# Block products in the down projection of the last four token tiles, and one scale per weight

## The chip, the cores and the metric

The kernel runs on one core of a Trainium2 chip. A core has a matrix engine (PE), a vector engine (DVE), an engine for functions (ACT), a general one (POOL) and one that mostly issues transfers (SP). Each works through its own list of instructions in order and waits, where it must, for what another engine or a transfer delivers. The metric is the device time of one execution in microseconds (us). Before the change it was 216.23 us, the median of three runs (215.68 to 216.25).

## The reference

The input x has S = 2048 tokens of D = 512 features. The kernel must give

```
xn  = layernorm(x)
out = x + linear_attention(xn) @ wo + ((xn @ w_gate) * (xn @ w_up)) @ w_down
```

in bfloat16. w_gate and w_up are 512 x 1792, w_down is 1792 x 512. The attention has 32 heads of 16 features: q, k and v come from wqkv; q and k pass a small matrix per head (w_phi) and become the feature map softmax(p) and softmax(-p); phi_k and v are summed over all tokens to one 32 x 17 block per head (the 17th column is the sum of phi_k); each token's phi_q times that block gives a numerator and a denominator, and their quotient goes through wo.

## The kernel before

The 2048 tokens are 16 tiles of 128, in groups of four. The 1792 hidden features are 14 slices of 128, the 512 features four. The code switches the framework's scheduler off: the order in which the code issues instructions is the order on each engine, transfers on SP among them.

The stages in time are these.

- *0 to about 88 us.* Layernorm and transposes; for the first eight tiles, gate and up are plain matmuls (`ffn`, L344 to L372), interleaved with the projections of k and v, their features and the sums KV. `weight_norm` (L417) has ACT sum the absolute values of each block of w_gate and w_up.
- *88 to 110 us.* `attend(n)` (L683) multiplies phi_q of tile n by KV into a PSUM bank `ab` that exists once; DVE then makes the denominator `den`, its reciprocal `rden` and the quotient `otok`, and SP transposes that to `oT`. `attend(n + 1)` cannot start until DVE has read `ab` of tile n. `qproj` makes q of a tile: PE's matmul, two exponentials on ACT, a reduction and a reciprocal on DVE (L300, L302), the product `phiq` on POOL (L304), and a transpose by SP. `fin(n)` (L374 to L406) is the last step of a tile: 14 rows (matmuls) with the slices of w_down and four with wo into one bank, then `store` adds x on DVE (L398) and sends the tile out.
- *110 to about 173 us.* Gate and up of tokens 1024 to 2047 are not plain products. For a pair of token groups and a pair of hidden slices, the 2 x 2 block product of activations and weights is made by seven block products in place of eight (`pair_block`, L467 to L540; `run_blocks`, L704). They need sums and differences of weights (`weight_sums`, L437, one 512-column subtraction each, on POOL or DVE, L445) and of tokens (`token_sums`, L449). Both are kept in fp16, so weights are first multiplied by a power of two (`weight_up`, L433), found from the norms in `weight_scales` (L422); `both` undoes it for each of seven pairs of slices. Block i (0 to 13) is gate or up of pair k. In a gate block, ACT copies partial sums out of PSUM with that scale (`keep`, L493) and DVE joins them (L499). In an up block ACT copies without scale (L495), DVE adds (L503) and the result is multiplied into the stored gate (L504): on POOL for the first six pairs, on DVE for the last. Rows of `fin` for tiles 4 to 7 and the q of tiles 7 to 12 fill PE between the products.
- *173 to 214 us.* The last block, then `fin` of tiles 8 to 15. Ahead of `fin(n)` for n = 9, 10, 11 stand q of tile n + 4 and `attend(n + 1)`. Tile 15 is done in two cuts, of 384 and 128 columns.

PSUM has eight banks: six turn over in one pool, and two are `ab` in the second and last stages, and banks for `fin` and q in the third.

The loop of the last stage sets the order around the change:

```
for n in range(9, NT):
    if n < 12:
        q_begin(n + 4, bank)
        q_rest()
    if n + 1 < NT:
        attend(n + 1, ps_ab)
    if sends:
        qsend()
    if n < 12:
        q_features(True)
    fin(n, cuts=(0, D) if n < NT - 1 else (0, 3 * P, D))
```

Of the kernel before, what the change touches and what calls it, by code (L numbers as in the profile page):

```python
# [23 lines left out]
def kernel(  # L24
# [49 lines left out]
    wgu = wpool.tile([P, 2, DC, F], BF16)  # L74
# [60 lines left out]
    xnT = xpool.tile([P, DC, HALF], BF16)  # L135
# [238 lines left out]
    def fin_parts(n, new_bank, lo=0, hi=D):  # L374
# [28 lines left out]
    def fin(n, cuts=(0, D)):  # L403
        for lo, hi in zip(cuts, cuts[1:]):
            for part in fin_parts(n, bank, lo, hi):
                part()  # L406

    nrm = consts.tile([P, FH, 2], BF16)
    up2 = consts.tile([P, FH, 2], F32)
    down2 = consts.tile([P, FH, 2], F32)  # L410
    both = consts.tile([P, FH], F32)
# [10 lines left out]
    def weight_scales():  # L422
        flat = lambda t: t[:].rearrange("p k g -> p (k g)")
        ps = bank("nrm")[:, 0:2 * FH]
        nc.tensor.matmul(ps, lhsT=ones[:, 0:P], rhs=flat(nrm), start=True, stop=True)
        nc.vector.tensor_scalar(out=flat(up2), in0=ps, scalar1=2.0 ** -40, scalar2=None, op0=ALU.max)
        nc.vector.tensor_scalar(out=flat(up2).bitcast(I32), in0=flat(up2).bitcast(I32), scalar1=0x7F800000,
                                scalar2=None, op0=ALU.bitwise_and)
        nc.vector.tensor_scalar(out=flat(down2), in0=flat(up2), scalar1=2.0 ** -14, scalar2=None, op0=ALU.mult)
        nc.vector.reciprocal(out=flat(up2), in_=flat(down2))  # L430
        nc.vector.tensor_tensor(out=both[:], in0=down2[:, :, 0], in1=down2[:, :, 1], op=ALU.mult)

    def weight_up(k, g):  # L433
        cols = pair_cols(k)[:, g]
        nc.scalar.activation(out=cols, in_=cols, func=AF.Identity, scale=up2[:, k, g:g + 1])  # L435
# [31 lines left out]
    def pair_block(k, g, new_bank):  # L467
# [7 lines left out]
        for t in range(2):  # L475
            T = NGRP // 2 + t
            if T not in hTs:
                hTs[T] = hpool.tile([P, FC, TT], BF16, name="hT", tag="h")
            for i in range(2):
                h[t, i] = hTs[T][:, k + i * FH, :]  # L480
        f = both[:, k:k + 1]
# [60 lines left out]
    norms = [(k, g) for k in range(FH) for g in range(2)]  # L542
# [61 lines left out]
    with tc.tile_pool(name="ps_k", bufs=1, space=PSUM) as ps_k:  # L604
# [66 lines left out]
        token_sums((0,))  # L671
        ffn(1)
        kv(NT - 2)
        ffn(1)
        kv(NT - 1)
        for b in range(2):
            nc.vector.tensor_tensor(out=KV[:, 4 * b:4 * b + 4, :, :], in0=kvps[b][:],
                                    in1=_bcast_ap(M4[:], [M4[:].ap[0], [0, 4], [E1, 4], [1, E1]]), op=ALU.mult)
        ffn(1)

    dpool = ctx.enter_context(tc.tile_pool(name="dp", bufs=2))

    def attend(n, ps_ab):  # L683
        ab = ps_ab.tile([P, 2, TT], F32, name="ab")
        for gr in range(NG):
# [6 lines left out]
                                scalar2=r2[:, n:n + 1] if n < GT else 1.0, op0=ALU.add, op1=ALU.mult)  # L692
# [11 lines left out]
    def run_blocks(lo, hi, first, second, third):  # L704
        for i in range(lo, hi):
# [7 lines left out]
            if 2 <= i < 2 * FH - 4:  # L713
                weight_up(*blocks[i + 4])
            new["p2"]()
# [12 lines left out]
    with tc.tile_pool(name="ps_ab", bufs=1, space=PSUM) as ps_ab:  # L728
        attend(0, ps_ab)
        weight_scales()  # L730
        qproj(4, True)
        token_sums((1,))
# [18 lines left out]
        qproj(7)  # L751
        weight_sums(1)
# [7 lines left out]
    with tc.tile_pool(name="ps_f", bufs=2, space=PSUM) as ps_f:  # L760
# [11 lines left out]

        def with_q(i):
# [4 lines left out]
                   lambda i: q_rest() if with_q(i) else filler(3 + i // 12))  # L778
        filler(len(fill))

    with tc.tile_pool(name="ps_ab2", bufs=1, space=PSUM) as ps_ab:
        nothing = lambda i: None
# [51 lines left out]
```

## Time and profile before

| | |
|---|---|
| median of three runs | 216.23 us |
| the profiled execution | 215.67 us |
| its span, first instruction to last | 213.9 us |
| clock granted to PE | 1.00 |
| busy: PE, DVE, ACT, POOL | 98%, 76%, 58%, 60% |
| `fin` with w_down, 238 matmuls | 54.1 us |
| transfers, share of 16 engines | 36.6% |

By stage, busy time in us:

| from, to | PE | DVE | ACT | POOL |
|---|---|---|---|---|
| 0 to 88 | 87.07 | 69.11 | 67.27 | 55.29 |
| 88 to 110 | 22.00 | 17.12 | 11.26 | 17.64 |
| 110 to 165 | 54.91 | 46.79 | 38.24 | 45.12 |
| 165 to 184 | 19.00 | 15.94 | 6.07 | 5.31 |
| 184 to 214 | 27.16 | 14.24 | 2.17 | 5.80 |

The profile is one execution, recorded by the hardware. A busy share says how much of the span an engine had an instruction running; the chain that ended last is followed back from the last instruction to whatever released each step. A line such as "0.42 DVE L445 TENSOR_TENSOR T<-wgu 128x512 f16<-128x512 bf16 x2" in a timeline names duration, engine, line of the kernel, operation, result and operands, their shapes and types, and how many instructions were merged. Matmuls overlap, so PE's rate is read from starts, not from durations.

### The profile page before, as it was taken

To read this page: it belongs to the slowest core of one execution; us is meant where nothing else is said; L and a number is where in the kernel's file an instruction comes from. 1 tells how busy PE (TensorE), PEld (TensorE's weight loads), DVE (VectorE), ACT (ScalarE), POOL (GpSimd) and SP (SyncE) were. 2 spreads that over 40 slices of the span, in tenths; PEclk is the share of its full clock that TensorE was granted. 3 is DMA by queue.
4 is the path that set the end of the run, shared out by engine and by line. 5 is a ranking of instruction groups with operands and counts; after the bars stand their busy time and mean duration, and the time that the engine had idled before them with its cause. 6 is when DMAs were issued, how large, how long until landed. Compare 5 with 4: busy or idle time off the path is not lost.

```text
span 213.9 us, 3610 instructions
## 1 busy us (share of the span) xinstructions
PE 210.1 (98%) x1280; PEld 101.7 (48%) x1280; DVE 163.2 (76%) x279; ACT 125.0 (58%) x219; POOL 129.2 (60%) x112
## 2 busy tenths in 40 slices
PE   8999999999999999999999999999999999999994
PEld 3664445444444444554444444444444444444543
DVE  5757979869867788887777897988969689776341
ACT  4635578998896999442666686868746352220000
POOL 3600557597895788859899497979788620333000
PEclk9999999999999999999999999999999999999999
DMA  5999995613022023234444202021120201333511
GB/s 152 266 281 385 374 287 87 91 26 75 0 51 52 0 49 81 66 40 112 100 101 100 49 0 52 0 74 25 48 49 3 74 26 34 91 98 98 126 49 49
DMA packets 47249, 19.91 MB, mean 93 GB/s; under 512 B 37504, under 2 KB 46976, under 8 KB 47104
## 3 DMA queue, kind: packets, MB, share of 16 engines
q1 hardware_dynamic: 47232, 19.69, 36.6%
q8 instruction: 10, 0.16, 0.3%
q14 instruction: 7, 0.06, 0.1%
HBM read 8.67 MB, written 2.10 MB: 50 GB/s over the span
## 4 chain that ended last, share of the span: by engine, by line
PE 98%; ACT 1%; DVE 0%; issue 0%
PE fin L387 29%; PE g L350 11%; PE u L350 11%; PE sa L487 11%; PE pv L285 7%; PE q L285 6%; PE k L285 6%; PE sc L487 6%; PE sb L487 3%; PE kv L622 2%; PE ab L686 2%; PE warm L554 2%; PE pq L272 1%; PE tp L253 1%; ACT k L493 0%; ACT xnT L256 0%
## 5 line engine op out<-in xcount | busy, mean ns | idle before, releaser
L387 PE MATMUL fin<-wd,hT 128*128 128x512 bf16 (+2 forms) x238 | 54.1, 366 | 0.0
L304 POOL TENSOR_TENSOR phiq<-e,rs 128x1024 bf16<-128x1024 f32 x16 | 30.9, 1934 | 25.6 <-DVE rs L302 18.1
L304 POOL TENSOR_TENSOR phik<-e,rs 128x1024 bf16<-128x1024 f32 x16 | 30.9, 1933 | 24.2 <-DVE rs L302 17.3
L300 DVE TENSOR_REDUCE sums<-e 128x64 f32<-128x1024 f32 x32 | 38.7, 1208 | 9.0 <-ACT e L296 9.0
L350 PEld LDWEIGHTS <-wgu 128*128 128x128 bf16 x240 | 23.1, 98 | 24.2
L387 PEld LDWEIGHTS <-hT 128*128 128x128 bf16 x238 | 22.3, 98 | 24.4
L350 PE MATMUL u<-xnT,wgu 128*128 128x512 bf16 (+1 forms) x120 | 29.1, 365 | 0.0
L350 PE MATMUL g<-xnT,wgu 128*128 128x512 bf16 (+1 forms) x120 | 28.9, 365 | 0.0
L504 POOL TENSOR_TENSOR hT<-u_sb,hT 128x512 bf16<-128x512 bf16 x18 | 21.1, 1185 | 10.1 <-DVE u_sb L503 10.1
L362 DVE TENSOR_TENSOR hT<-u,g_sb 128x512 bf16<-128x512 f32 (+1 forms) x30 | 18.6, 622 | 4.5 <-PE u L350 3.9
L356 ACT CAST g_sb<-g 128x512 bf16<-128x512 f32 (+1 forms) x30 | 17.1, 569 | 8.1 <-PE g L350 7.9
L294 ACT ACTIVATE e<-q 128x512 f32<-128x512 f32 x12 | 7.2, 598 | 23.6 <-PE q L285 23.6
L302 DVE RECIPROCAL rs<-sums 128x64 f32<-128x64 f32 x32 | 17.7, 552 | 2.5
L493 ACT ACTIVATE k<-sa,both 128x512 f32<-128x512 f32 x21 | 14.5, 688 | 8.7 <-PE sa L487 8.6
L495 ACT COPY k<-sa 128x512 f32<-128x512 f32 x21 | 12.3, 587 | 11.2 <-DVE u_sb L503 7.4
L398 DVE TENSOR_TENSOR o_sb<-fin,xall 128x512 bf16<-128x512 f32 (+2 forms) x13 | 8.4, 646 | 12.0 <-PE fin L387 12.0
L445 POOL TENSOR_TENSOR T<-wgu,T 128x512 f16<-128x512 bf16 x14 | 17.0, 1216 | 0.5
L387 PE MATMUL fin<-wo,oT 128*128 128x512 bf16 (+2 forms) x68 | 17.1, 366 | 0.0
L487 PEld LDWEIGHTS <-T 128*128 128x128 f16 x112 | 10.8, 98 | 13.1 <-issue 0.6
L487 PE MATMUL sa<-ss,T 128*128 128x512 f16 x56 | 16.7, 379 | 0.1
L435 ACT ACTIVATE wgu<-wgu,up 128x1024 bf16<-128x1024 bf16 x14 | 15.9, 1156 | 0.1
L420 ACT ACTIVATE junk<-wgu 128x1024 bf16<-128x1024 bf16 x14 | 15.1, 1083 | 0.0
(98 smaller groups left out, 352.1 us busy)
## 6 DMA issues: line engine op xcount, KB each, us to landing
out_dram<-o_sb SPq DMA_DIRECT2D x15, 128.0 KB, 1.9
wd<-in_B_w_down_dram SPq DMA_DIRECT2D x1, 1792.0 KB, 15.4
wgu<-in_B_w_gate_dram SPq DMA_DIRECT2D x2, 640.0 KB, 6.8
wgu<-in_B_w_up_dram SPq DMA_DIRECT2D x2, 640.0 KB, 8.0
xall<-in_A_x_dram SPq DMA_DIRECT2D x1, 1024.0 KB, 12.1
xall<-in_A_x_dram SPq DMA_DIRECT2D x4, 128.0 KB, 2.7
vk<-in_A_wqkv_dram SPq DMA_DIRECT2D x2, 256.0 KB, 3.6
wgu<-in_B_w_gate_dram SPq DMA_DIRECT2D x2, 256.0 KB, 4.9
```

The lines of the kernel that those rows point to most:

```text
L285: nc.tensor.matmul(ps, lhsT=xt(n)[:, j, :], rhs=w[:, j, :], start=(j == 0), stop=(j == DC - 1))
L300: nc.vector.tensor_reduce(out=sums[:], in_=ev, axis=AX.X, op=ALU.add)
L302: nc.vector.reciprocal(out=rs[:].rearrange("p a b -> p (a b)"), in_=sums[:])
L304: nc.gpsimd.tensor_tensor(out=phi[:].rearrange("p g (x f) -> p (g x) f", f=DH), in0=ev, in1=rs[:].to_broadcast((P, 2 * H, DH)), op=ALU.mult)
L350: nc.tensor.matmul(ps, lhsT=w[:, c, f * P:(f + 1) * P], rhs=xnT[:, c, T * TT + lo:T * TT + hi], start=(c == 0), stop=(c == DC - 1))
L356: nc.scalar.copy(out=g_sb[:, 0:n], in_=ps)
L362: nc.vector.tensor_tensor(out=hTs[T][:, f, lo:hi], in0=ps, in1=g_sb[:, 0:hi - lo], op=ALU.mult)
L387: nc.tensor.matmul(held[0], lhsT=rows[i][0], rhs=rows[i][1], start=(i == 0), stop=(i == len(rows) - 1))
L435: nc.scalar.activation(out=cols, in_=cols, func=AF.Identity, scale=up2[:, k, g:g + 1])
L445: (nc.gpsimd if i % 2 or k < 2 else nc.vector).tensor_tensor(out=t[:, i], in0=a, in1=b, op=ALU.subtract)
L487: nc.tensor.matmul(held[name], lhsT=w[:, j, :], rhs=x[:, j, :], start=start and j == 0, stop=(j == hc - 1), skip_group_check=True)
L504: (nc.vector if k == FH - 1 else nc.gpsimd).tensor_tensor(out=dst, in0=u[:], in1=dst, op=ALU.mult)
```

## The change

*w_down of tiles 12 to 15.* They are taken as two pairs, (12, 13) and (14, 15). For a pair, the activations are a 2 x 2 block matrix (two tiles by two halves of the 1792 hidden features), w_down another (two halves of the hidden features by two halves of its 512 columns). The product is made by seven block products of seven matmuls with 256 columns each (`down_pair`, p1 to p7, p2 of the last pair in halves p2a and p2b, plus `w22`, which has only rows of wo) and 16 rows of wo, in place of two `fin`.

*What the products need.* All quarters of w_down in fp16, multiplied by a power of two (`scaled`, on ACT, 12 pieces of 768 or 1024 columns, six in blocks 5 to 10 and six in and after the last block); four differences of quarters (`minus`, 16 pieces of 512 or 256 columns, all on POOL: one at block 10, three at 11, four at 12, the rest in the last stage); and four sums or differences of activations per pair (`hidden_sums`, 896 columns each; number 0 and number 6 on POOL, the others on DVE). Inside `down_pair`, `keep` copies partial sums on ACT, `add` adds x or another partial sum on POOL, and `join` finishes a half tile on DVE. The new tiles lie where tiles that are no longer read were: the first w_down pieces over the transposed activations of the first half and over x of tiles 0 to 3, the activation sums over w_gate and w_up.

*Scales.* Gate times up of tokens 1024 to 2047 is stored in fp16 with a fixed factor (`gate_scale`), so the seven factors `both` become one constant. Each weight has one scale, from the root of its sum of squares: `weight_norm` takes squares, with seven more calls for w_down, and `weight_roots`, `weight_scales` and `product_scales` replace the old `weight_scales`. The factors are undone in `store`, in `den` (`scale_of`) and in `down_pair`.

*Order.* q of tile 13 stands ahead of the last two rows of `fin(8)`; three rows of `fin(9)` ahead of `attend(10)`; q of 14 behind `fin(9)`; q of 15 in the middle of `fin(10)`. `attend(14)` and `attend(15)` stand inside the first pair. The first of `token_sums` stands two units of `ffn` later.

```diff
...
-            if n < GT:
-                nc.vector.scalar_tensor_tensor(out=o_sb[:], in0=ps, scalar=r2[:, n:n + 1], in1=xres,
-                                               op0=ALU.mult, op1=ALU.add)
+            if n < GT or n >= QT:
+                nc.vector.scalar_tensor_tensor(out=o_sb[:], in0=ps, scalar=r2[:, n:n + 1] if n < GT else inv_a[:],
+                                               in1=xres, op0=ALU.mult, op1=ALU.add)
             else:
                 nc.vector.tensor_tensor(out=o_sb[:], in0=ps, in1=xres, op=ALU.add)
             nc.sync.dma_start(out=out_view(n, n + 1)[:, 0, lo:lo + w], in_=o_sb[:])
...
     def weight_norm(k, g):
-        junk = xnpool.tile([P, DC, 2, P], BF16, name="junk", tag="x")
+        junk = xnpool.tile([P, 1024], BF16, name="junk", tag="x")
+        cols = pair_cols(k)[:, g] if g < 2 else wd[:, 2 * k:2 * k + 2, :]
+        out = junk[:].rearrange("p (c h f) -> p c h f", c=DC, h=2) if g < 2 else junk[:].rearrange("p (c f) -> p c f", c=2)
         with nc.allow_low_precision(reason="a bound for a power of two"):
-            nc.scalar.activation(out=junk[:], in_=pair_cols(k)[:, g], func=AF.Abs, accum_out=nrm[:, k, g:g + 1])
-
...
+            nc.scalar.activation(out=out, in_=cols, func=AF.Square, accum_out=nrm[:, g, k:k + 1])
...
+    def weight_roots(lo, hi):
+        n = hi - lo
+        ps = bank("nrm")[:, 0:n * FH]
+        nc.tensor.matmul(ps, lhsT=ones[:, 0:P], rhs=nrm[:, lo:hi, :].rearrange("p g k -> p (g k)"), start=True, stop=True)
+        f, u = fro[:, lo:hi], up3[:, lo:hi]
+        nc.vector.tensor_reduce(out=f, in_=ps.rearrange("p (g k) -> p g k", g=n), axis=AX.X, op=ALU.add)
+        nc.gpsimd.tensor_scalar(out=f, in0=f, scalar1=2.0 ** -60, scalar2=None, op0=ALU.max)
+        nc.gpsimd.tensor_tensor(out=u, in0=f, in1=mhalf[:, 0:n], op=ALU.pow)
+
+    def weight_scales(lo, hi):
+        u = up3[:, lo:hi]
+        nc.vector.tensor_scalar(out=u.bitcast(I32), in0=u.bitcast(I32), scalar1=0x7F800000,
                                 scalar2=None, op0=ALU.bitwise_and)
-        nc.vector.tensor_scalar(out=flat(down2), in0=flat(up2), scalar1=2.0 ** -14, scalar2=None, op0=ALU.mult)
-        nc.vector.reciprocal(out=flat(up2), in_=flat(down2))
-        nc.vector.tensor_tensor(out=both[:], in0=down2[:, :, 0], in1=down2[:, :, 1], op=ALU.mult)
+        nc.vector.tensor_scalar(out=u, in0=u, scalar1=levels[lo], scalar2=None, op0=ALU.mult)
+        nc.vector.reciprocal(out=down3[:, lo:hi], in_=u)
+
+    def product_scales():
+        nc.vector.scalar_tensor_tensor(out=inv_a[:], in0=down3[:, 0:1], scalar=levels[0] * levels[1] / hidden_scale,
+                                       in1=down3[:, 1:2], op0=ALU.mult, op1=ALU.mult)
+        nc.vector.tensor_tensor(out=inv_ab[:], in0=inv_a[:], in1=down3[:, 2:3], op=ALU.mult)
...
-        f = both[:, k:k + 1]
+        f = gate_scale
...
+    def scaled(dst, quarter):
+        def piece(lo, hi):
+            nc.scalar.activation(out=dst[:, lo:hi], in_=quarters[quarter][:, lo:hi], func=AF.Identity, scale=up3[:, 2:3])
+
+        return [lambda p=p: piece(*p) for p in PIECES]
...
+    def minus(dst, a, b):
+        def piece(eng, lo, hi):
+            eng.tensor_tensor(out=dst[:, lo:hi], in0=a[:, lo:hi], in1=b[:, lo:hi], op=ALU.subtract)
+
+        return [lambda eng=nc.gpsimd, p=p: piece(eng, *p) for p in SMALL]
...
+    def down_early():
+        t = npool.tile([P, 16, W], F16, name="dT", tag="xnT")
+        down["t1"], down["t2"] = t[:, 0:FH], t[:, FH:2 * FH]
+        down["b11"] = xall[:, 0:GT, :].rearrange("p n (j f) -> p (n j) f", f=W)[:, 0:FH]
+        for name in ("t1", "t2", "b11"):
+            blocks_of(name.upper(), down[name])
+        return (scaled(down["b11"], "11") + scaled(down["t1"], "12") + scaled(down["t2"], "22"),
+                minus(down["t1"], down["t1"], down["b11"]) + minus(down["t2"], down["t2"], down["t1"]))
...
+    def down_late():
+        t = hpool.tile([P, 4, FH, W], F16, name="dT2", tag="h")
+        t3, t4, b22, b21 = (t[:, i] for i in range(4))
+        for name, v in (("T3", t3), ("T4", t4), ("B22", b22), ("B21", b21)):
+            blocks_of(name, v)
+        return (scaled(t3, "12") + scaled(b21, "21") + scaled(b22, "22"),
+                minus(t3, b22, t3) + minus(t4, b21, down["t2"]))
...
+    def hidden_sums():
+        t = gupool.tile([P, 4, 4, FH, P], F16, name="dS", tag="wgu")
+        todo = []
+        for i, n in enumerate(outer):
+            a11, a12, a21, a22 = (hcols(m, lo, lo + FH) for m in (n, n + 1) for lo in (0, FH))
+            for j, (a, b, op) in enumerate(((a21, a22, ALU.add), (t[:, i, 0], a11, ALU.subtract),
+                                            (a11, a21, ALU.subtract), (a12, t[:, i, 1], ALU.subtract))):
+                todo.append(lambda eng=nc.vector, dst=t[:, i, j], a=a, b=b, op=op:
+                            eng.tensor_tensor(out=dst, in0=a, in1=b, op=op))
+            for j in range(4):
+                down[n, f"S{j + 1}"] = [t[:, i, j, k, :] for k in range(FH)]
+        return todo
+
...
+        S = [down[n, f"S{j + 1}"] for j in range(4)]
+        held = {}
...
+        inv = inv_ab[:]
+        keeps = [xnpool.tile([P, 2, W], F32, name="dK", tag="x") for _ in range(2)]
+        k1, k2, k3, k5 = (keeps[i][:, j, :] for i in range(2) for j in range(2))
...
+        def product(name, a, b, lo=0, hi=W, start=True, wo_of=None):
+            if name not in held:
+                held[name] = new_bank("d" + name)
+            ps = held[name][:, lo:hi]
+            rows = [(a[k], b[k][:, lo:hi]) for k in range(FH)]
+            if wo_of:
+                rows += attn(*wo_of, lo, hi)
+            run(ps, rows, start)
+
+        def attn(m, half, lo=0, hi=W):
+            return [(oTs[m][:, c, :], wo[:, c, half * W + lo:half * W + hi]) for c in range(DC)]
+
+        def run(ps, rows, start):
+            for i, (l, r) in enumerate(rows):
+                nc.tensor.matmul(ps, lhsT=l, rhs=r, start=start and i == 0, stop=(i == len(rows) - 1),
+                                 skip_group_check=True)
...
+        def keep(dst, name):
+            nc.scalar.activation(out=dst, in_=held[name][:, 0:W], func=AF.Identity, scale=inv)
+
+        def add(dst, b):
+            nc.gpsimd.tensor_tensor(out=dst, in0=dst, in1=b, op=ALU.add)
+
+        def join(m, half, name, b, lo=0, hi=W):
+            if m not in o_sb:
+                o_sb[m] = opool.tile([P, D], BF16, name=f"o_sb{D}", bufs=3)
+            nc.vector.scalar_tensor_tensor(out=o_sb[m][:, half * W + lo:half * W + hi], in0=held[name][:, lo:hi],
+                                           scalar=inv, in1=b, op0=ALU.mult, op1=ALU.add)
...
+        def p1():
+            product("a", A(n, 0), down["B11"])
+            keep(k1, "a")
+            add(k1, x(n, 0))
+
+        def p2(lo=0, hi=W):
+            name = f"b{lo}"
+            product(name, A(n, FH), down["B21"], lo, hi, wo_of=(n, 0))
+            join(n, 0, name, k1[:, lo:hi], lo, hi)
+            if last:
+                send(n, lo, hi)
+
+        def p5():
+            product("d", S[0], down["T1"])
+            keep(k5, "d")
+
+        def p6():
+            product("a", S[1], down["T2"], start=False)
+            keep(k2, "a")
+            add(k2, x(n, 1))
+            add(k2, k5)
+
+        def p3():
+            product("c", S[3], down["B22"], wo_of=(n, 1))
+            join(n, 1, "c", k2)
+            send(n, W if last else 0)
+
+        def p7():
+            product("a", S[2], down["T3"], start=False)
+            keep(k3, "a")
+            add(k3, x(n + 1, 1))
+
+        def w22():
+            run(held["d"][:, 0:W], attn(n + 1, 1), False)
+            join(n + 1, 1, "d", k3)
+
+        def p4():
+            product("a", A(n + 1, FH), down["T4"], start=False, wo_of=(n + 1, 0))
+            join(n + 1, 0, "a", x(n + 1, 0))
+            send(n + 1)
+
+        return dict(p1=p1, p2=p2, p3=p3, p4=p4, p5=p5, p6=p6, p7=p7, w22=w22, p2a=lambda: p2(0, P), p2b=lambda: p2(P, W))
...
             if n >= 12:
                 qproj(n - 12)
             norm(2 if n < 6 else 1)
+        ffn(1)
+        kv(NT - 2)
+        ffn(1)
         token_sums((0,))
...
+        weight_roots(0, 2)
         ffn(1)
...
+    def scale_of(n):
+        return r2[:, n:n + 1] if n < GT else 1.0 if n < QT else inv_a[:] if n < outer[0] else inv_ab[:]
...
-                                scalar2=r2[:, n:n + 1] if n < GT else 1.0, op0=ALU.add, op1=ALU.mult)
+                                scalar2=scale_of(n), op0=ALU.add, op1=ALU.mult)
...
+            if i == 3:
+                weight_roots(2, 3)
+            if i == 4:
+                weight_scales(2, 3)
+                product_scales()
...
-        weight_scales()
+        norm(1)
         qproj(4, True)
+        weight_scales(0, 2)
...
+        norm(2)
...
+        norm(2)
...
+        norm(2)
...
+        copies, dsum = down_early()
...
-                   lambda i: q_rest() if with_q(i) else filler(3 + i // 12))
+                   lambda i: (q_rest() if with_q(i) else filler(3 + i // 12),
+                              [c() for c in take(copies, i, {5: 1, 6: 1, 7: 1, 8: 1, 9: 1, 10: 1})],
+                              [d() for d in take(dsum, i, {10: 1, 11: 3, 12: 4})]))
         filler(len(fill))
...
+        copies, late = down_late()
+        dsum += late
...
+        run_blocks(2 * FH - 1, 2 * FH, lambda i: None, lambda i: attend(8, ps_ab), lambda i: None)
         state["old"]["p7"]()
+        some(copies, 2)
...
         state["old"]["p3"]()
+        hsum = hidden_sums()
         filler(2)
+        some(copies, 4)
         attend(9, ps_ab)
+        hsum[0](nc.gpsimd)
+        some(dsum, 4)
+        filler(len(fill) - 2)
+
...
+        q_next(13)
         filler(len(fill))
-        for n in range(9, NT):
-            if n < 12:
-                q_begin(n + 4, bank)
-                q_rest()
...
-                q_features(True)
-            fin(n, cuts=(0, D) if n < NT - 1 else (0, 3 * P, D))
+        fin(9, part=(0, 3))
+        attend(10, ps_ab)
+        q_features(True)
+        fin(9, part=(3, FC + DC))
+        q_next(14)
+        attend(11, ps_ab)
+        qsend()
+        q_features(True)
+        some(dsum, 2)
+        fin(10, part=(0, 9))
+        q_next(15)
+        qsend()
+        q_features(True)
+        fin(10, part=(9, FC + DC))
+        some(dsum, 2)
+        attend(12, ps_ab)
+        qsend()
+        for part in hsum[1:4]:
+            part()
+        fin(11)
+        attend(13, ps_ab)
+        new = [down_pair(n, bank, n == outer[-1]) for n in outer]
+        parts(new[0], "p1", "p5", "p6", "p2")
+        attend(14, ps_ab)
+        hsum[4]()
+        parts(new[0], "p7", "p3")
+        attend(15, ps_ab)
+        hsum[6](nc.gpsimd)
+        hsum[5]()
+        hsum[7]()
+        parts(new[0], "w22", "p4")
+        parts(new[1], "p1", "p5", "p6", "p3", "p7", "p2a", "w22", "p4", "p2b")
...
```

More of the change, by code (lines that the diff above doesn't have):

```diff
@@ L401, in fin_parts, with fin @@
         return [lambda i=i: mm(i) for i in range(FC + DC)]
[L403 to L411, printed above, removed]
+    open_fins = {}
+    def fin(n, part=(0, FC + DC)):
+        if n not in open_fins:
+            open_fins[n] = fin_parts(n, bank)
+        for i in range(*part):
+            open_fins[n][i]()
+    nrm = consts.tile([P, 3, FH], BF16)
+    fro = consts.tile([P, 3], F32)
+    up3 = consts.tile([P, 3], F32)
+    down3 = consts.tile([P, 3], F32)
+    inv_a = consts.tile([P, 1], F32)
+    inv_ab = consts.tile([P, 1], F32)
+    levels = (8.0, 8.0, 4096.0)
+    hidden_scale = 16.0
+    gate_scale = hidden_scale / (levels[0] * levels[1])
     Ts = {}
@@ L674 @@
         ffn(1)
+        token_sums((0,))
         kv(NT - 1)
@@ L771, in filler, with take @@
                 fill.pop(0)()
+        copies, dsum = down_early()
+        def take(todo, i, plan):
+            return [todo.pop(0) for _ in range(plan.get(i, 0))]
         def with_q(i):
```

54 lines of the change are left out of this document (35 added, 19 removed).

## The prediction

> **What bounds the kernel now.** I read the page's shares first, then the chain that ended last, then the timeline by engine in the stretches that the diff touches, and last the rows of the operations that it adds.
>
> ```profile
> span 213.9 us, 3610 instructions
> PE 210.1 (98%) x1280; PEld 101.7 (48%) x1280; DVE 163.2 (76%) x279; ACT 125.0 (58%) x219; POOL 129.2 (60%) x112
> PE 98%; ACT 1%; DVE 0%; issue 0%
> 12.16 0.60 PE L350 MATMUL u<-xnT,wgu 128*128 128x256 bf16 x4
> 12.60 0.60 PE L350 MATMUL g<-xnT,wgu 128*128 128x256 bf16 x4
> ...
> 90.19 1.03 PE L350 MATMUL u<-xnT,wgu 128*128 128x512 bf16 x4
> 91.06 0.42 PE L686 MATMUL ab<-KV,phiqT 128*128 128x68 bf16 x8
> ...
> 209.99 0.94 PE L387 MATMUL fin<-wd,hT 128*128 128x128 bf16 x14
> 210.72 0.27 PEld L387 LDWEIGHTS <-oT 128*128 128x128 bf16 x4
> 210.77 0.39 PE L387 MATMUL fin<-wo,oT 128*128 128x128 bf16 x4
> ```
>
> The first three lines say that PE's work is the time: 98% of the chain, and no other engine over 76%. So every matmul column removed is time won, unless PE comes to wait. The timeline lines give the pitch from start to start (the durations overlap): 512 columns (90.19 to 91.06)/4 = 0.216 us, 256 columns 0.44/4 = 0.109, 128 columns 0.78/14 = 0.056. Narrow matmuls keep the full rate here, and eight 68-column ones of attend take 0.25.
>
> ```profile
> 122.85 1.71 DVE L445 TENSOR_TENSOR T<-wgu 128x512 f16<-128x512 bf16 x2
> 123.01 1.27 POOL L504 TENSOR_TENSOR hT<-u_sb,hT 128x512 bf16<-128x512 bf16 x1 [1.42 <-DVE u_sb L503]
> ...
> L445 POOL TENSOR_TENSOR T<-wgu,T x14: 1148/1155/1333, 107.9 to 163.7; 128x512 f16<-128x512 bf16 x14
> L445 DVE TENSOR_TENSOR T<-wgu x10: 414/894/1378, 122.8 to 161.2; 128x512 f16<-128x512 bf16 x10
> L504 DVE TENSOR_TENSOR hT<-u_sb,hT x3: 424/424/425, 174.1 to 178.7; 128x512 bf16<-128x512 bf16 x3
> ```
>
> These are the lines that decide. A DVE tensor_tensor of two SBUF tensors takes 0.41 alone; of the two at 122.85 the second takes up to 1.38. The pair ends at 124.56, just 0.28 after POOL's multiplication, which began between them (123.01 + 1.27 = 124.28). So the second stood until POOL's instruction was over, and POOL, which had waited behind the first, went in before the second. The three of L504 stay at 0.42, as POOL does nothing from 172.3 to 184.1.
>
> **The change, part by part** (times are those of the profile before).
>
> *Removed from PE.* Tiles 12 to 14 cost 18 x 0.216 = 3.88 each, tile 15 in two cuts 18 x (0.1625 + 0.056) = 3.93 (384 columns: 162.5 ns from 207.06 to 209.34 over 14): 15.58. Each pair now has 7 x 7 products and 16 rows of wo, 65 x 0.109 = 7.09; the last pair's p2 in halves adds 0.03. 15.58 - 14.20 = **-1.38**. The weight-norm matmuls (14 columns before; 14 and 7 now) are nothing.
>
> *Constant scale in blocks.* L493 with a scale operand takes 0.69, the exponentials with a constant 0.60. PE stood 0.08 and 0.25 in block 0 (113.56, 114.93) for that ACT result; 0.09 off each keep leaves 0.16: **-0.17**. Below nothing is left to win later: PE has no other gap over 0.03 from there on.
>
> *Seven norms of w_down on ACT* (Square; as L420, pitch 1.04) and the w_gate/w_up scales a little later. One lies in the idle 88.1 to 89.6. Two behind each of q 5, 6, 7: ACT ends them at 99.6, 104.6 and 109.8, w_gate/w_up scaling follows to 106.7 and 111.9, so the gate copy starts 0.3 late, and the first keep of block 0 (112.82) is not touched. Cover: ACT's idle 3.2, 3.9 and 1.9. If Square cost 0.2 more each, block 0 would start about 0.5 late; taken as 0. The roots and scales are a dozen DVE and POOL operations of 0.1 to 1.0 (L426 to L431, L176) in blocks with 1 us of DVE idle: 0, at most 0.3.
>
> *Six scalings of w_down on ACT in blocks 5 to 10* (L435's 1.04 pitch, 0.78 for 768): odd blocks have 0.72 idle ahead of the first keep plus 0.18 from the constants, even ones 1.2 to 1.5; p6 needs that keep only 0.9 later. 0. The six late ones run 175.3 to 180.8, and the exponential of q 13 was at 180.75: 0.
>
> *POOL.* 16 subtractions (512 columns: 1.15, pitch 1.11; 256: 0.67, by 1.9 ns a column between L445 and L454's 1024 in 2.12), two sums of 896 (1.88), eight adds of 256 (0.67). They fill the idle 172.3 to 184.1 entirely, and that cover of DVE is gone. Adding them in order: one at 162.25 pushes T to 166.0 (needed at 167.9), phiq 12 to 168.2; then hT, three pieces, hT, hT to 174.41, four pieces, dS.
>
> **Wait 1, blocks to fin.** DVE's three L504 now meet POOL. The first (due 174.13) waits for hT's end: done 174.69, +0.14. The second, due 177.1, waits for a subtraction that ends at 177.9: +0.7. L510 behind it ends at 178.8, and that is what POOL's dS waits for: it starts 178.9 and ends 180.8. DVE's third L504, ready at 179.45, waits for it: 181.05 instead of 179.14. The last row of fin(8) reads it. PE, which now does q 13 first, wants that row at 180.27: 0.8 lost. Queued behind on DVE: den, rden, otok of tile 9 (1.2), done 182.3; attend(10) needs the bank, and PE is there at 181.96: 0.35 more. **+1.2**. Bounds: 0 if DVE gets in before dS; 2.2 if the first L504 loses the race at 174.3 to the next piece (then oT of tile 8 is 1 us late).
>
> *Queues in between.* SP's transposes and stores keep their order but for tile 13's phiq; oT(9) lands 184.7 for 184.9. phiq 13, 14 come 1 to 2 us late for attends with 4 to 5 us to spare.
>
> **Wait 2, ahead of attend(14).** From the end of q 15 on PE (call it 0): fin(10)'s second half 1.94, attend(12) 0.25, fin(11) 3.88, attend(13) 0.25, p1, p5, p6 (0.76 each), p2 (1.20): PE wants attend(14) at 9.8. DVE: exponentials of q 15 at +1.4, reduction and reciprocal to 3.2, store(10) 0.75, then den, rden, otok of tile 12 to 5.1; then three differences of 896. Price of one: 0.42 at least (L504's 512), 1.2 at most (as a PSUM operand's 691 for 512); 0.63 by L504's rate, the value nearest in kind. Alone they end at 6.85; store(11), den, rden, otok of tile 13 take 2.0 more: 8.8, in time by 1.0. But POOL at that point has phiq 15 (4.9 to 6.85, since phiq 14 and two pieces come first) and then two pieces. Alternating as at 122.85: difference, piece, difference, piece, difference end at 7.3, 8.35, 8.8, 9.35, 9.8; otok(13) at 11.7. **+1.95** (bounds 0 and 2.6). That phiq excludes DVE as L504 does isn't in the rows; it is the same operation on POOL, with both inputs in SBUF, so I take it so.
>
> The Trainium skill (SBUF — State Buffer, Who interferes with whom) states that a Vector instruction with two SBUF inputs and a GpSimd instruction that reads SBUF exclude each other, the second one blocking fully. By that rule phiq blocks as well and the sum stands; without it, wait 2 falls within its spare 1.0 and the sum is 1.95 less.
>
> *Pair 2.* Its sums on DVE meet POOL's adds and dS too: otok(14) 0.45 ahead of attend(15), S2 0.6 ahead of its product: 0. Keeps (0.46 with operand at 256, by L493 less half a cast) end 0.05 ahead of p6. In the no-wait case this is the next to be late.
>
> *End.* The last join is 0.35 for 0.29, and 128 KB are sent 0.4 ahead of the last 32 KB (before: 96 KB, 0.7 ahead): **+0.15** (0 to 0.4).
>
> Sum: -1.38 - 0.17 + 1.2 + 1.95 + 0.15 = **+1.75**. The profiled execution took 215.67 (span 213.9 and 1.8 around it), 0.56 under the median 216.23; I carry the difference to the median: 218.0.
>
> **The rivals.**
> - *Faster: DVE is not held.* Place: the three differences behind otok(12), and the third L504. It decides at 1.0 us of lateness for the former and 1.1 for the latter. For it: no trace row shows phiq against such a DVE operation, and POOL's spans may be shorter. Against: five of five meetings in blocks held DVE. Both waits gone: 216.23 - 1.40 = 214.8.
> - *One wait only.* Wait 1 alone: 216.0; wait 2 alone: 216.8.
> - *More waits:* the race at 174.3, or pair 2's sums late: 218.8 to 219.5.
> - *The seven products save nothing*, because 256 columns don't keep the rate: +0; the pitches 0.109 and 0.056 exclude it.
>
> **How the numbers follow.** Both waits 0.50 (own range 217.3 to 218.7), more 0.08, none 0.27, wait 1 alone 0.08, wait 2 alone 0.07. Under 0.3% (0.65 us) this kernel's runs tell nothing from no change, so the bounds are 215.6 and 216.9: faster 0.27, same 0.15, slower 0.58. The range is 214.5 to 219.0. Below it has the no-wait case with the tail at 0 and both gaps of block 0 gone whole (216.23 - 1.38 - 0.33 = 214.5); above, the upper end of the likeliest and the lower half of more waits.
>
> **What would show it.** Right: PE gaps of about 0.8 at fin(8)'s last row, 0.35 ahead of attend(10) and 2 ahead of attend(14); the third multiplication by u_sb on DVE near 1.6 us instead of 0.42; the sums dS on DVE over 1 us each while POOL is busy; matmuls of 256 columns at 0.109. Wrong: those DVE rows at 0.42 and 0.63 beside a busy POOL, and PE without gaps: then the whole 1.4 us is won.

## The result and the profile after

The changed kernel takes 218.75 us (median of four runs, 218.50 to 219.16), the kernel before 215.95 (215.49 to 216.25) on the same chip. The ratio is 1.0133, with a 95% interval of 1.0104 to 1.0163: slower by 2.8 us. The forecast was 218.0 in a range of 214.5 to 219.0, slower with a chance of 0.58.

The profiled execution took 219.16, with a span of 217.4 (before: 215.67 and 213.9). So the spans differ by 3.5 and the medians by 2.8: this execution is 0.41 over its median, and that of before 0.28 under its own.

From the page of the changed kernel, the span, the busy shares, and the chain that ended last:

```profile
span 217.4 us, 3801 instructions
PE 210.2 (97%) x1332; PEld 106.4 (49%) x1332; DVE 174.4 (80%) x294; ACT 144.5 (66%) x253; POOL 157.8 (73%) x142
PE 78%; DVE 12%; ACT 3%; issue 3%; DMA 2%; POOL 1%; ACTq 0%; DVEq 0%
```

Before, PE was 98% of the chain. Now DVE has 12% of it. POOL has grown by 28.6 us of work, yet is 1% of the chain: what POOL costs is seen on DVE. Below, a DVE instruction is called *held* when it could run but stands until an instruction of POOL is over; its row is then longer than the same instruction takes alone.

The timeline at the first wait of the forecast, the end of the blocks (start, duration, engine, line, operation, times; a wait and its releaser in brackets):

```profile
174.81 4.19 POOL L582 TENSOR_TENSOR dT<-dT 128x512 f16<-128x512 f16 x4
174.81 1.44 DVE L526 TENSOR_TENSOR hT<-u_sb,hT 128x512 f16<-128x512 bf16 x1
...
176.74 1.46 PE L389 MATMUL fin<-wd,hT 128*128 128x512 bf16 x6
...
178.76 0.53 DVE L526 TENSOR_TENSOR hT<-u_sb,hT 128x512 f16<-128x512 bf16 x1
178.78 0.59 PE L509 MATMUL sc<-ss,wgu 128*128 128x512 f16 x2 [0.58 <-DVE u_sb L525]
...
180.06 1.88 POOL L617 TENSOR_TENSOR dS<-hT 128x896 f16<-128x896 f16 x1 [1.05 <-PE ab L859]
...
180.52 1.70 DVE L526 TENSOR_TENSOR hT<-u_sb,hT 128x512 f16<-128x512 bf16 x1
```

The multiplication that took 0.42 before (L504, now L526) takes 1.44, 0.53 and 1.70. The first becomes ready as POOL's subtractions begin and stands until the first of them is over; the six rows of fin ahead of p3 end at 176.74 + 6 x 0.216 = 178.04, and p3 starts at 178.78: PE stands for 0.74. The third stands until POOL's sum is over (180.06 + 1.88 = 181.94).

And the timeline at the second wait, ahead of attend(14):

```profile
195.77 1.94 POOL L306 TENSOR_TENSOR phiq<-e,rs 128x1024 bf16<-128x1024 f32 x1
196.00 2.19 DVE L617 TENSOR_TENSOR dS<-dS,hT 128x896 f16<-128x896 f16 x1
...
197.66 2.55 POOL L582 TENSOR_TENSOR dT<-dT,dT 128x512 f16<-128x512 f16 x2
...
198.11 1.57 DVE L617 TENSOR_TENSOR dS<-hT 128x896 f16<-128x896 f16 x1
...
199.60 1.09 DVE L617 TENSOR_TENSOR dS<-hT,dS 128x896 f16<-128x896 f16 x1
...
200.45 0.60 PE L648 MATMUL db<-wo,oT 128*128 128x256 bf16 x4
...
201.93 0.69 DVE L869 TENSOR_TENSOR otok<-ab,rden 128x512 bf16<-128x512 f32 x1
...
202.77 0.41 PE L859 MATMUL ab<-KV,phiqT 128*128 128x68 bf16 x8 [1.72 <-DVE otok L869]
```

The three differences take 2.19, 1.57 and 1.09, where the same instruction later takes 0.61. Each ends 0.5 after the POOL instruction that ran when it became ready, phiq first. The four rows of wo end at 200.45 + 4 x 0.109 = 200.89 and attend(14) starts at 202.77: PE stands for 1.88.

### The profile page after: what moved, and what is told of

It reads as the page before. It is cut to its first block, busy times and chain, and to the rows that moved or that the text cites. A ratio compares the mean times of both kernels' runs of the same rounds, so it can differ in the third digit from the quotient of the medians.

```text
span 217.4 us, 3801 instructions
## 1 busy us (share of the span) xinstructions
PE 210.2 (97%) x1332; PEld 106.4 (49%) x1332; DVE 174.4 (80%) x294; ACT 144.5 (66%) x253; POOL 157.8 (73%) x142
## 4 chain that ended last, share of the span: by engine, by line
PE 78%; DVE 12%; ACT 3%; issue 3%; DMA 2%; POOL 1%; ACTq 0%; DVEq 0%
PE fin L389 14%; PE g L352 11%; PE u L352 11%; PE sa L509 8%; PE pv L287 7%; PE k L287 6%; PE q L287 5%; PE sc L509 4%; PE da L648 3%; PE sb L509 2%; PE kv L791 2%; DMA oT<-otok 2%; DVE hT L526 2%; DVE dS L617 2%; PE warm L723 1%
## 5 line engine op out<-in xcount | busy, mean ns | idle before, releaser
L389 PE MATMUL fin<-wd,hT 128*128 128x512 bf16 x168 | 41.5, 379 | 0.1
L352 PEld LDWEIGHTS <-wgu 128*128 128x128 bf16 x240 | 23.2, 98 | 24.2
L526 POOL TENSOR_TENSOR hT<-u_sb,hT 128x512 f16<-128x512 bf16 x18 | 21.1, 1187 | 8.0 <-DVE u_sb L525 8.0
L389 PEld LDWEIGHTS <-hT 128*128 128x128 bf16 (+1 forms) x168 | 16.1, 98 | 19.3 <-DVE hT L526 0.6
L515 ACT ACTIVATE k<-sa 128x512 f32<-128x512 f32 x21 | 12.6, 600 | 7.3 <-PE sa L509 7.1
L287 PEld LDWEIGHTS <-x 128*128 128x128 f16 x96 | 9.1, 98 | 10.2
L509 PEld LDWEIGHTS <-wgu 128*128 128x128 bf16 x84 | 8.1, 98 | 10.7 <-issue 1.5
```

Source lines behind the costliest of these rows:

```text
L287: nc.tensor.matmul(ps, lhsT=xt(n)[:, j, :], rhs=w[:, j, :], start=(j == 0), stop=(j == DC - 1))
L352: nc.tensor.matmul(ps, lhsT=w[:, c, f * P:(f + 1) * P], rhs=xnT[:, c, T * TT + lo:T * TT + hi], start=(c == 0), stop=(c == DC - 1))
L389: nc.tensor.matmul(held[0], lhsT=rows[i][0], rhs=rows[i][1], start=(i == 0), stop=(i == len(rows) - 1))
L509: nc.tensor.matmul(held[name], lhsT=w[:, j, :], rhs=x[:, j, :], start=start and j == 0, stop=(j == hc - 1), skip_group_check=True)
L526: (nc.vector if k == FH - 1 else nc.gpsimd).tensor_tensor(out=dst, in0=u[:], in1=dst, op=ALU.mult)
```

## The experiments

All are compared with the kernel before on the same chip; losses of PE are read from starts, as above, and the names of the sums are those of the diff.

**No subtractions.** Twelve of POOL's sixteen subtractions are left out; the scaled quarters go into the products in their place.

```diff
-                minus(down["t1"], down["t1"], down["b11"]) + minus(down["t2"], down["t2"], down["t1"]))
+                minus(down["t1"], down["t1"], down["b11"]))
...
-        for name, v in (("T3", t3), ("T4", t4), ("B22", b22), ("B21", b21)):
+        for name, v in (("T3", t3), ("T4", b21), ("B22", b22), ("B21", b21)):
...
-        return (scaled(t3, "12") + scaled(b21, "21") + scaled(b22, "22"),
-                minus(t3, b22, t3) + minus(t4, b21, down["t2"]))
+        return (scaled(t3, "12") + scaled(b21, "21") + scaled(b22, "22"), [])
...
-                              [d() for d in take(dsum, i, {10: 1, 11: 3, 12: 4})]))
+                              [d() for d in take(dsum, i, {10: 1, 11: 3})]))
...
```

> This kernel leaves out twelve of POOL's sixteen subtractions of w_down quarters (those of T2, four of them behind block 12, and all of T3 and T4 in the last stage); the products read the scaled quarters in their place, so the amount of matmul, DVE and ACT work stays and only POOL's load goes. Theory (a POOL subtraction holds a DVE instruction with two SBUF operands): the first multiplication by u_sb of the last block falls from 1.44 to about 0.45 us, PE's 0.74 gap ahead of p3 of that block goes; the third still stands behind POOL's first activation sum, so 0.1 to 0.8 us stays around attend(10); the three activation differences on DVE meet only phiq of tile 15 and take about 2 us in place of 4.85, so the 1.89 ahead of attend(14) goes. Time 215.7 to 216.4. Rival (DVE's queue is too long by its own work, and POOL's subtractions lie beside it): both gaps stay and the time is 218.3 to 219.

215.35 us, ratio 0.998 (0.9968 to 0.9991). The timeline of this kernel, at the first multiplication, at the third, and at the three differences:

```profile
174.30 0.42 DVE L526 TENSOR_TENSOR hT<-u_sb,hT 128x512 f16<-128x512 bf16 x1
...
178.43 1.88 POOL L616 TENSOR_TENSOR dS<-hT 128x896 f16<-128x896 f16 x1 [4.09 <-DMA oT<-otok]
...
178.95 1.64 DVE L526 TENSOR_TENSOR hT<-u_sb,hT 128x512 f16<-128x512 bf16 x1
...
192.74 1.93 POOL L306 TENSOR_TENSOR phiq<-e,rs 128x1024 bf16<-128x1024 f32 x1 [0.78 <-issue]
...
194.37 0.79 DVE L616 TENSOR_TENSOR dS<-dS,hT 128x896 f16<-128x896 f16 x1
...
195.08 0.61 DVE L616 TENSOR_TENSOR dS<-hT 128x896 f16<-128x896 f16 x1
...
195.61 0.61 DVE L616 TENSOR_TENSOR dS<-hT,dS 128x896 f16<-128x896 f16 x1
```

Both large losses of PE are gone, with all of DVE's and PE's own instructions still there. DVE has the time for its own work; it was POOL's load that made it late. Of the first wait, the part behind POOL's sum stays (1.64; PE loses 0.07 and 0.49 around attend(10)). The time is below the expected 215.7.

**First sum on DVE.**

```diff
-        hsum[0](nc.gpsimd)
+        hsum[0](nc.vector)
```

> The first activation sum of pair 12/13 goes from POOL to DVE, behind the quotient of tile 9. Theory: the third multiplication by u_sb, which stood 1.70 us beside POOL's sum, falls to about 0.45 to 0.55, the gaps of 0.31 and 0.49 around attend(10) go, the 0.74 of the first one and the 1.89 ahead of attend(14) stay: about 0.8 less, 217.7 to 218.3. Rival (the sum only changes queues, DVE now being late by it): attend(10) or a later attend waits as long, 218.5 to 219.5.

218.08, ratio 1.0107 (1.0086 to 1.0128). From the timeline of this kernel, the third multiplication and the sum:

```profile
180.31 0.43 DVE L526 TENSOR_TENSOR hT<-u_sb,hT 128x512 f16<-128x512 bf16 x1
...
181.93 0.62 DVE L617 TENSOR_TENSOR dS<-hT 128x896 f16<-128x896 f16 x1
```

The third multiplication takes 0.43, and PE's 0.31 and 0.49 around attend(10) are gone; 0.73 (first multiplication) and 1.83 (attend(14)) stay. The sum itself took 0.62 on DVE against 1.88 on POOL.

**Scale as an operand.** Two products of one element per partition.

```diff
-        nc.vector.scalar_tensor_tensor(out=inv_a[:], in0=down3[:, 0:1], scalar=levels[0] * levels[1] / hidden_scale,
-                                       in1=down3[:, 1:2], op0=ALU.mult, op1=ALU.mult)
-        nc.vector.tensor_tensor(out=inv_ab[:], in0=inv_a[:], in1=down3[:, 2:3], op=ALU.mult)
+        nc.vector.tensor_scalar(out=inv_a[:], in0=down3[:, 0:1], scalar1=down3[:, 1:2],
+                                scalar2=levels[0] * levels[1] / hidden_scale, op0=ALU.mult, op1=ALU.mult)
+        nc.vector.tensor_scalar(out=inv_ab[:], in0=inv_a[:], scalar1=down3[:, 2:3], scalar2=None, op0=ALU.mult)
```

> The two one-element products inv_a and inv_ab in block 4 are written with the second factor as the per-partition scalar of the instruction, not as its second SBUF operand; same values, same place, same engine. In the changed kernel they took 0.64 and 1.08 us beside POOL's two multiplications, and PE lost 0.53 in blocks 4 and 5. Theory (what is held is a second SBUF operand streamed by DVE): 0.1 to 0.2 us each, PE's 0.53 goes, time 218.0 to 218.4, the gaps of the last stage as they were. Rival (the lateness is that of the whole chain of scale operations, which waits for POOL's power): they stay near 1 us or PE's loss stays over 0.3, time 218.5 to 219.

218.25, ratio 1.0119 (1.0094 to 1.0144). First the changed kernel's groups of these lines (minimum, median and maximum in ns, start in us), then those of this kernel:

```profile
L451 DVE SCALAR_TENSOR_TENSOR inv_a<-down x1: 644/644/644, 130.7 to 130.7; 128x1 f32<-128x1 f32 x1
L453 DVE TENSOR_TENSOR inv_ab<-inv_a,down x1: 1078/1078/1078, 131.4 to 131.4; 128x1 f32<-128x1 f32 x1
```

```profile
L451 DVE TENSOR_SCALAR inv_a<-down x1: 195/195/195, 130.4 to 130.4; 128x1 f32<-128x1 f32 x1
L453 DVE TENSOR_SCALAR inv_ab<-inv_a,down x1: 214/214/214, 130.7 to 130.7; 128x1 f32<-128x1 f32 x1
```

In both kernels POOL runs two multiplications at that time. With the factor as the instruction's scalar, DVE is not held, and PE's losses in blocks 4 and 5 (0.13, 0.17 and 0.24) are gone. The chain of scale operations was not late by itself.

**Scales alone.** The new scales and fp16 gate times up, with `fin` of tiles 12 to 15 as before.

```diff
...
-        parts(new[0], "p1", "p5", "p6", "p2")
...
+        for n in range(9, NT):
...
+            for lo, hi in ((0, D),) if n < NT - 1 else ((0, 3 * P), (3 * P, D)):
+                for part in fin_parts(n, bank, lo, hi):
+                    part()
```

> Half of the change alone: one scale per weight with its norms and roots, and fp16 gate times up, but w_down of tiles 12 to 15 and the order of the last stage as before the change; no scaled quarters, subtractions or activation sums. Theory: PE's gaps of the last stage are gone, its 1.38 of work is back, 0.5 us of loss stays in block 4 and up to 0.3 near 94.7, block 0 wins under 0.1: 216.3 to 216.8, slower than before by 0.2 to 0.4%. Rival (the fp16 results or the new scales slow the last stage themselves): 217 or more, with gaps behind block 13.

216.18 against 215.69, ratio 1.0024 (1.0014 to 1.0034). PE's only new losses are the 0.53 of blocks 4 and 5, and block 0 wins 0.06: together 0.47, and 0.49 is measured. The last stage has none. The time is just below the expected 216.3: the loss near 94.7, of up to 0.3, did not occur.

**Two differences later.** The second and third difference go behind the quotient of tile 13.

```diff
-        for part in hsum[1:4]:
-            part()
+        hsum[1]()
         fin(11)
         attend(13, ps_ab)
+        hsum[2]()
+        hsum[3]()
```

> Only this is changed against the changed kernel: the second and third of the three activation differences stand behind the quotient of tile 13 on DVE and not ahead of it; POOL's work and its order stay. Theory: attend(14) waited because otok(13) stood behind differences that POOL held up, so with one of three ahead otok(13) ends near 200.3 and the 1.89 goes; p7 and p3 of the first pair then wait up to 0.5 together for the two sums. 216.9 to 217.6, 1.2 to 1.9 less. Rival (whatever waits, the three differences must be done before PE can go on, so the wait moves to p7): a gap of over 1.2 ahead of p7 or p3, 218 to 219.

218.87, ratio 1.016 (1.014 to 1.0179): nothing won. My number was wrong; the time is that of the rival, though not at the place that it named (over 1.2 ahead of p7 or p3). The 1.88 ahead of attend(14) is gone, and came back as 0.10 ahead of p3, 0.55 ahead of attend(15) and 1.19 in the second pair. The timeline of this kernel there:

```profile
203.03 1.88 POOL L617 TENSOR_TENSOR dS<-hT 128x896 f16<-128x896 f16 x1
203.27 2.12 DVE L617 TENSOR_TENSOR dS<-hT 128x896 f16<-128x896 f16 x1
...
206.97 1.08 DVE L617 TENSOR_TENSOR dS<-dS,hT 128x896 f16<-128x896 f16 x1
...
208.11 0.61 PE L648 MATMUL da<-dT,dS 128*128 128x256 f16 x4 [1.03 <-DVE dS L617]
```

In the changed kernel DVE's first sum of pair 14/15 began at 204.50, ahead of POOL's third at 205.61, and took 0.61. Here POOL's began 0.24 ahead of DVE's, and DVE's took 2.12. The hold explains that; I had not followed the shift to the next meeting.

**The same, with POOL's sum on DVE,** to see whether it was this one instruction (the edit above and `hsum[6]()` in place of `hsum[6](nc.gpsimd)`).

> As the kernel with two of the three differences behind the quotient of tile 13, which lost 0.10 ahead of p3, 0.55 ahead of attend(15) and 1.19 ahead of the second pair's p6 in place of 1.89 ahead of attend(14); and the second pair's sum that stood on POOL is made by DVE. There it had begun 0.24 us before DVE's first sum of that pair, which took 2.12 in place of 0.61. Theory (the loss was given back to this one instruction of POOL): the 1.19 goes and 0.5 to 0.7 is left, 217.4 to 217.9. Rival (DVE is late by its own queue, the sums pushed back): the 1.19 stays within 0.3, 218.5 to 219.

217.69, ratio 1.0082 (1.0067 to 1.0098). The 1.19 is gone, 0.09 and 0.55 are left. So it was.

**One operand on POOL.** The subtractions become multiplications by 1, in the same place.

```diff
-            eng.tensor_tensor(out=dst[:, lo:hi], in0=a[:, lo:hi], in1=b[:, lo:hi], op=ALU.subtract)
+            eng.tensor_scalar(out=dst[:, lo:hi], in0=a[:, lo:hi], scalar1=1.0, scalar2=None, op0=ALU.mult)
```

> POOL's sixteen subtractions are replaced by multiplications of their first operand by 1, one SBUF operand in place of two (the differences of w_down quarters are left out, the order and the sizes are kept). By the layernorm's 0.77 for such an instruction of 512 columns, the pieces get shorter. Theory (any POOL instruction that reads SBUF holds DVE's two-operand ones): the first multiplication by u_sb takes about 1.1 to 1.3 in place of 1.44, the three differences still alternate with the pieces, the gap ahead of attend(14) falls from 1.89 to 0.6 to 1.2: 217.2 to 218. Rival (two operands on each side are needed for the hold): multiplications at 0.42 to 0.53, differences at 0.61 behind phiq, both gaps gone, 216 to 216.6.

216.09, ratio 1.0027 (1.0018 to 1.0036): the rival's time, though not both gaps are gone. From the timeline of this kernel, at the multiplications and at the differences:

```profile
176.12 5.21 POOL L582 TENSOR_SCALAR dT<-dT 128x512 f16<-128x512 f16 x4
...
177.64 0.82 DVE L526 TENSOR_TENSOR hT<-u_sb,hT 128x512 f16<-128x512 bf16 x1
...
179.69 0.43 DVE L526 TENSOR_TENSOR hT<-u_sb,hT 128x512 f16<-128x512 bf16 x1
...
192.11 2.93 POOL L582 TENSOR_SCALAR dT<-dT 128x512 f16<-128x512 f16 x2
...
194.16 0.61 DVE L617 TENSOR_TENSOR dS<-dS,hT 128x896 f16<-128x896 f16 x1
...
194.69 0.62 DVE L617 TENSOR_TENSOR dS<-hT 128x896 f16<-128x896 f16 x1
...
195.02 2.08 POOL L306 TENSOR_TENSOR phiq<-e,rs 128x1024 bf16<-128x1024 f32 x1
...
195.22 2.36 DVE L617 TENSOR_TENSOR dS<-hT,dS 128x896 f16<-128x896 f16 x1
...
197.06 1.86 POOL L582 TENSOR_SCALAR dT<-dT 128x512 f16<-128x512 f16 x1
```

Beside POOL's one-operand instructions DVE's take 0.61, 0.62 and 0.43, and once 0.82; beside phiq, with two operands, 2.36. This does not show that a one-operand instruction never holds DVE. The multiplication of 0.82 began 0.07 after the POOL instruction beside it, the three rows that were not longer began 0.59 or more after theirs; so the hold may cover only the first part of a one-operand instruction, and no run tests that. The other way round it is there: POOL's one-operand instruction at 197.06 took 1.86 in place of 1.48, beside the difference that ended at 197.58. The one-operand instructions are not shorter, as I had expected from the layernorm's 0.77: 1.48 for 512 columns against 1.15 for the subtraction. PE keeps 0.62 ahead of attend(14) and 0.44 ahead of attend(15), the first behind the difference that phiq held.

**Combined.** The complete computation, with each wait met at its place.

The two products with a scale operand are as above. The other edits:

```diff
-                (nc.vector if k == FH - 1 else nc.gpsimd).tensor_tensor(out=dst, in0=u[:], in1=dst, op=ALU.mult)
+                nc.gpsimd.tensor_tensor(out=dst, in0=u[:], in1=dst, op=ALU.mult)
...
-                              [d() for d in take(dsum, i, {10: 1, 11: 3, 12: 4})]))
+                              [d() for d in take(dsum, i, {10: 1, 11: 3})]))
...
+        some(dsum, 1)
         state["old"]["p7"]()
...
-        hsum[0](nc.gpsimd)
+        hsum[0]()
...
-        for part in hsum[1:4]:
-            part()
+        hsum[1]()
+        some(dsum, 1)
         fin(11)
         attend(13, ps_ab)
+        hsum[2]()
+        hsum[3]()
...
```

So the twelve subtractions that are left after block 11 are issued on POOL as follows: one between the first two multiplications of block 13, four behind `attend(9)`, two ahead of phiq of tile 14 and one behind it, one behind phiq of tile 15, one behind the first difference, and one each behind p1 and p6 of the first pair.

> The changed kernel, complete, with each of its waits met at its place: the two one-element products with a scale operand; the last block's three multiplications by u_sb on POOL as those of the other blocks; the first activation sum on DVE; T2's four subtractions taken out of block 12, one put between the first two multiplications of block 13 and the rest, with T3's and T4's, spread over POOL's idle time between the phiq of tiles 13 to 15 and the adds of the first pair; of the three activation differences only the first ahead of the quotient of tile 13, the other two behind it. Theory: all of PE's 0.53, 1.66 and 1.89 of loss goes, 218.75 less about 4 is 214.3 to 214.9, faster than before by 0.4 to 0.7%. Rival (DVE and POOL together have no room for this work in the last stage: each wait put away comes back at the next product or attend): gaps of 1 us or more remain behind attend(12), 215.5 to 217.

214.83 against 215.51, ratio 0.9968 (0.9955 to 0.998): faster than both kernels. PE still loses 0.26 ahead of attend(15), 0.11 and 0.31 in the second pair, each behind a sum of DVE that stands beside POOL.

**All sums on DVE.** As combined, and also:

```diff
...
-        some(dsum, 4)
+        some(dsum, 5)
...
-        hsum[6](nc.gpsimd)
+        hsum[6]()
...
```

A second subtraction also stands between block 13's multiplications, and with these two the rest come earlier: the last two follow phiq of tile 15.

> The combined version with two more steps: the second pair's third activation sum (1.88 us on POOL) goes to DVE too, and two more of POOL's subtractions stand in its idle time before the phiq of tile 13, so that the last of T4 is done before the first pair's adds. In the combined version PE still lost 0.26 ahead of attend(15), 0.11 and 0.31 in the second pair's products. Theory (these are DVE's sums behind POOL's instructions): all three go, 0.5 to 0.7 less, 214.0 to 214.5. Rival (DVE has no room left for one more sum in the last pair): the loss in the second pair stays or grows, 214.8 or more.

214.81 against 215.66, ratio 0.9957 (0.9943 to 0.9971). The 0.26 is gone, but the second pair still loses 0.07 and 0.35, so the rival was right in the time. Its reason, that DVE has no room, fits only the 0.07, which is behind a sum that took 0.62. The 0.35 is one more hold: POOL's add of x (0.67) now runs beside the last of DVE's sums, which took 1.09. This is not shown to be faster than the combined version: the medians are alike and the intervals of the two ratios overlap.

## Why the prediction was right, and where it was not

It held in its mechanism and by its main terms, with the sizes below (PE's losses of the profiled execution, from starts). The size was too small: the change was forecast at +1.75 and is +2.8 in the medians. That 218.0 lies within 0.75 of the measured time is in part luck, as it starts from a median of 216.23, where that of the comparison is 215.95. The likeliest case had a range of its own, 217.3 to 218.7, and 218.75 lies just above it. What happened at the first wait is what the rival "more waits" named (the race at 174.3, 218.8 to 219.5), with a chance of 0.08.

| term | forecast | measured |
|---|---|---|
| PE's work | -1.38 | -1.37 |
| constant scale, block 0 | -0.17 | -0.06 |
| norms, roots and scales | 0, at most 0.3 | +0.53 |
| wait 1 | +1.2 (0 to 2.2) | +1.66 |
| wait 2 | +1.95 (0 to 2.6) | +1.88 |
| end | +0.15 (0 to 0.4) | +0.51 |
| not in the sum: `fin(0)` waits at 94.7 | 0 | +0.30 |

The measured terms add up to 3.45, the spans differ by 3.5.

*PE's work* came as worked out: 256 columns at 0.109 from start to start, 128 at 0.056.

*Wait 1* had the right mechanism, shown by the first two experiments, but the race went the other way: the first multiplication lost it to the next subtraction. The forecast had that as its upper bound, but with the loss at oT of tile 8. That cost only 0.13; the 0.74 came before it, at p3, which waited for DVE to read a partial sum (`u_sb`). So 0.74 and 0.13 were lost near p3, and 0.31 and 0.49 in place of 0.8 and 0.35 behind POOL's sum.

*Wait 2* is right in its place, its order (phiq, piece, piece between the differences) and its size. That phiq holds DVE, which the forecast assumed without a row, is shown by 2.19 here and by 2.36 beside it in the one-operand kernel. The price of one difference, 0.63 "by L504's rate", is less than 0.424 for 512 columns gives in proportion (0.74), and the forecast doesn't say how it comes; alone, one took 0.61. The rule cited ahead of the result (the Trainium skill, SBUF — State Buffer, Who interferes with whom) agrees for POOL's instructions with two operands. For one-operand instructions, which also read SBUF, it would have DVE wait as well, until they are over; there the runs differ (0.61, 0.62 and 0.43 not held, once 0.82), and the measurement decides.

*Roots and scales* is the step that failed: "a dozen DVE and POOL operations of 0.1 to 1.0 ... in blocks with 1 us of DVE idle", put at 0, at most 0.3. I applied the hold to large instructions only. Two of the dozen have two SBUF operands, though of one element, and stood for 0.64 and 1.08 beside POOL's multiplications, and PE lost 0.53 behind them.

*Block 0*: the copies did get 0.09 shorter (0.69 to 0.60), but PE's two waits there went only from 0.33 to 0.27. The copies still end both waits, PE going on 0.05 after each. But they begin later: 0.48 and 0.47 after the start of the last row that they wait for, where it was 0.42 before. So only 0.03 of each 0.09 is won. Why they begin later there, and not from 121 us on (0.42 again), stays open.

*The end* was mis-sized: 3.28 from PE's last matmul to the end of the span in place of 2.77. The step that the forecast priced, the last join and the last transfers, is not where it went: the last store landed 1.89 after PE's last matmul, where it was 1.84 before. The other 0.45 lies behind that landing, where nothing of the computation is left: from there to the end of the span it took 1.39 in place of 0.93. In the eight other kernels with the same last pair that rest is 1.01 (without subtractions, combined, and with all sums on DVE) or 1.37 to 1.46, without an edit that explains it. That stays open.

*The 0.30 at 94.7* is a wait for the transpose of oT of tile 0. Transposes between 88 and 110 us took 3.3 to 3.9 here and 2.4 to 2.7 before (medians from issue to landing). Of the nine kernels run afterwards, which all have this part of the change, one shows 0.30 there, one 0.09 and seven nothing. The transposes of phiq are long in all nine (3.6 to 3.9), so the wait can come in each of them, but mostly does not. So I don't count it to the change; it may be part of why this execution is slower than its median.

The rival "DVE is not held" is refuted by the rows above. That the combined kernel ends at its time (214.83 for 214.8) is luck: the rival was to win 1.40 over the kernel before, and the combined kernel wins 0.68 over the 215.51 of its comparison; PE still stands for 0.68 there.

## What to carry to other kernels

An instruction moved to an engine with idle time is not free when that engine shares something with a busier one: read a row in which both run, and look for one that ends just after the other's. Then follow each shifted instruction to its next meeting, as a delay put away in one place came back some 5 us later with one more meeting. A small instruction can be held as long as a large one, and here the cure was to give the second factor as the instruction's scalar.

## What the runs showed that was not expected

A DVE product of one element per partition took 1.08 us as tensor_tensor and 0.21 as tensor_scalar with the second factor as its scalar, both beside POOL's multiplications. A POOL multiplication of 512 fp16 columns by a constant took 1.48, longer than the subtraction of two such tensors (1.15), and yet cost DVE's two-operand instructions nothing in three meetings, in which they began 0.59 or more after it, and 0.4 in one, which began 0.07 after it.
